# A hand-ordered list of steps in a fused mLSTM and channel-mix kernel: filling operand made first, first row fetched right behind its store, copies of unit 4's keys put behind chunk 7's scores and two row fetches

## The chip, the cores and the metric

The kernel runs on one core of one Trainium2 chip. A core has a matrix engine (PE), three engines for elementwise work (DVE, ACT, POOL) and a queue engine (SP) that here only issues transfers; ACT issues some transfers too. Each engine works through its own instructions in order and waits on semaphores that other engines and transfers raise. The metric is device microseconds of one execution, and the median over the runs is compared.

## The reference

Two layers follow each other. The first is an mLSTM over 4 batches, 8 heads, 768 steps and a head dimension of 40; the second is a channel mix on its output, with d_model 320 and d_ff 1024.

```python
m_new = np.maximum(f_gate[:, :, t] + m, i_gate[:, :, t])
f_stab = np.exp(f_gate[:, :, t] + m - m_new)
i_stab = np.exp(i_gate[:, :, t] - m_new)
C = f_stab[:, :, None, None] * C + i_stab[:, :, None, None] * np.einsum('bhd,bhe->bhde', vt, kt)
n = f_stab[:, :, None] * n + i_stab[:, :, None] * kt
h_tilde = np.einsum('bhde,bhe->bhd', C, qt)
denom = np.maximum(np.abs(nq), 1.0)          # nq = n . q
y[:, :, t] = sigmoid(o_gate) * h_tilde / denom
...
xk = mu_k * x + (1.0 - mu_k) * x_prev
xr = mu_r * x + (1.0 - mu_r) * x_prev
k = np.maximum(xk @ w_k, 0.0)
v = k * k @ w_v
out = sigmoid(xr @ w_r) * v
```

## The kernel before

The sequence is cut into 12 units of 256 tokens (3 for each batch) and each unit into 2 chunks of 128, so that there are 24 chunks. Within a chunk the mLSTM is a masked product: `scores` (line 471) multiplies keys by queries on PE, `exps` (464) makes the decay weights on ACT from a row that was fetched and masked, `weigh` (479) multiplies the two on DVE, and `intra` (504) multiplies the result by the values on PE. The state between chunks goes through `keys` (553), `carry` (568), `carry_out` (579) and `inter` (483). The channel mix of a unit is `turn` and `mix`, then `ffn_k`, `relu`, `sq`, `ffn_v` and `ffn_r`, each in float32 that is split into two parts, so that a product takes several matmuls.

All work is recorded in one list, `ORDER` (lines 51 to 203): each entry is a function's name and its arguments, a trailing letter naming the engine or queue (V is DVE, G POOL, A ACT, S SP). The order of the entries is the order of the instructions on every engine; no scheduler changes it. Transfers therefore stand in SP's row in the order of the list as well.

The steps that the prediction speaks of:

- `work` (296) writes the operand `busy` on DVE; `fill v n` (288) issues n matmuls of `busy` by `busy` whose result nobody reads. `zeros` (240) clears 32 rows of the buffers `k_first` and `q_first` on DVE.
- The gate scans of a segment c of 128 steps are `gate_b` (327), `gate_m` (338) and `gate_n` (349) on DVE, with `scale_a`, `scale_k` and `scale_d`. `turn_g` (369) transposes their rows on PE and `cols` (378) turns them into columns on ACT.
- `store_n c` (353) writes the row of segment c to a scratch tensor `nm` in device memory. `fetch_m g` (453) reads it back, 8 heads spread over all 128 partitions (512 KB), into one of two buffers `e`; `mask` (459) blanks the upper triangle on POOL. Segment c serves the chunks c, c+6, c+12 and c+18.
- The weights come by `load_w` (643), in four buffers, and go through `w_size` (650, ACT), `w_guard` and `w_bits` (657, 662, DVE), `w_h` (673, ACT) and `w_l` (677).
- `load_n`, `load_v`, `load_x`, `load_qs`, `load_o`, `load_cm` fetch a unit's keys, values, stacked queries or keys, gates, and the block mask of `carry_out`.
- Units 0 to 3 read keys and queries straight from `k_first` and `q_first`. From unit 4 on the stacks `k3` and `q3` are put together by `restack` (439): for the keys six copies of the high part (`restack u k h`), three of the low part (`k l`), and the same for the queries, 18 copies from buffer to buffer for a unit, all issued by SP. `k3` and `q3` have one buffer each, the same that `k_first` and `q_first` lie in, so unit 4's copies wait for the last scores of unit 3 (`scores 7 1`).

Of the kernel before, what the change touches and what calls it, by code (L numbers as in the profile page):

```python
# [14 lines left out]
B, H, S, D = 4, 8, 768, 40  # L15
# [33 lines left out]


ORDER = """
zeros V; consts; edge 0; load_i S; load_f A; gate_b 0; scale_a 0 G; load_w wk 0 A; gate_m 0; gate_n 0;
scale_k 0 V; load_n 0 S; blank; store_n 0 S; gate_b 1; work; load_w wk 1 A; gate_r 0; gate_i 1 V; gate_m 1;
scale_a 1 V; load_v 0 A; gate_n 1; scale_d 1 V; store_n 1 S; fill v 20; turn_g 0; cols 0; gate_r 1;
scale_k 1 G; fill v 13; turn_g 1; w_size wk 0; w_guard wk 0 V; w_bits wk 0 0; w_bits wk 0 1; w_bits wk 0 2;
load_mu A; gate_b 2; gate_i 2 V; gate_m 2; scale_a 2 G; gate_b 3; keys 0 G; gate_n 2; scale_d 2 V; cols 1;
keys 1 V; gate_r 2; gate_i 3 V; gate_m 3; load_x 0 q S; scale_k 2 V; gate_n 3; fill v 42; carry 0; load_cm S;
carry_out 0; w_size wk 1; scale_a 3 V; scale_k 3 V; fill v 10; carry 1; carry_out 1; fetch_m 0 S; fetch_m 1 S;
mask 0; w_h wk 0; exps 0 0; load_x 0 k S; w_l wk 0 V; store_n 2 S; w_guard wk 1 V; w_bits wk 1 0;
w_bits wk 1 1; fill v 6; turn_g 2; load_w wk 2 S; load_w wk 3 A; cols 2; carry_old 1 V; load_n 1 S; load_v 1 S;  # L60
gate_r 3; gate_b 4; gate_i 4 V; scale_a 4 G; fill v 10; scores 0 1; store_n 3 S; exps 0 1; scale_d 3 G;
load_o 0 S; gate_m 4; gate_n 4; scale_k 4 G; store_n 4 S; turn_g 3; cols 3; weigh 0 1; w_size wk 2; fill v 10;
scores 0 0; mask 1; exps 1 1; weigh 0 0; fill v 7; intra 0 0; gate_r 4; intra 0 1; w_bits wk 1 2; scores 1 0;
w_guard wk 2 V; w_bits wk 2 0; w_bits wk 2 1; w_bits wk 2 2; scores 1 1; scale_d 4 V; carry_add 1 V; keys 2 V;
load_qs 0 S; gate_b 5; gate_i 5 V; gate_m 5; fill v 10; carry 2; scale_a 5 V; carry_old 2 V; fetch_m 2 S;
gate_n 5; scale_k 5 G; inter 1; mask 2; w_h wk 1; w_h wk 2; exps 1 0; total 0; inter_v 1; w_size wk 3;
# [19 lines left out]
w_h wr 1; sq_l 0 0; turn 3; turned 3; mask 6; scores 6 0; w_guard wv 2 V; w_bits wv 2 0; w_l wr 0 V; intra 5 1;  # L86
w_l wr 1 V; scores 6 1; exps 6 0; weigh 6 0; change 1 G; load_qs 3 S; inter_v 5; total 5; exps 6 1; weigh 6 1;
norm 2 0; ffn_k 0 2; ffn_r 0 0; tanh_r 0 0; load_x 4 q S; split_h 4 q; sq_h 0 1; load_v 3 S; w_bits wv 2 1;
w_bits wv 2 2; intra 6 0; intra 6 1; load_o 2 S; norm 2 1; sq 0 1 A; restack 4 k h S; keys 7 V; scores 7 0;
norm 2 2; split_l 4 q V; carry 6; fetch_m 7 S; carry_out 6; ffn_r 0 1; mask 7; total 6; sq_l 0 1; mix 1 k;  # L90
tanh_o 2; sig_o 2; gate 2 G; outcome 2 G; restack 4 k l S; edge 2; tanh_r 0 1; fetch_m 8 S; scores 7 1;
exps 7 0; weigh 7 0; exps 7 1; weigh 7 1; ffn_k 0 3; relu 0 2; sq_h 0 2; mask 8; inter 7; inter_v 7; intra 7 0;
restack 4 q h S; restack 4 q l S; sq 0 2 V; load_n 4 A; twin 2; w_size wv 3; intra 7 1; total 7; norm 3 0;
norm 3 1; sq_l 0 2; load_v 4 S; w_guard wv 3 V; turn 4; mix_h 1 k; ffn_v 0 0 0; ffn_v 0 0 1; turned 4;
# [743 lines left out]
```

## Time and profile before

| | us |
|---|---|
| median of 3 runs | 394.19 |
| the three runs | 388.84, 394.19, 396.33 |
| the profiled execution, whole time | 396.55 |
| its span, first to last instruction | 394.8 |

| engine | busy us | share of the span |
|---|---|---|
| PE matmul | 359.2 | 91% |
| DVE | 273.5 | 69% |
| ACT | 220.5 | 56% |
| POOL | 114.8 | 29% |

PE's busy time contains the fillings, and it contains matmuls that ran while a lower clock was granted. The page cuts the span in 40 slices; the row of the granted clock stands in tenths, 9 being full.

```profile
PEclk9998967996759987999999999999999999999999
```

The slices with 5 to 8 lie in the first 160 us. After that the clock is full, and PE is nearly always busy.

### The profile page before, as it was taken

The page shows a single profiled execution, that of the slowest core. Times are in us where ns is not written, and L with a number is a line of the kernel's source. Part 1 is how long each engine was busy: PE and PEld are TensorE (multiplying, and loading weights), DVE is VectorE, ACT ScalarE, POOL GpSimd, SP SyncE. Part 2 cuts the span into 40 slices and gives each one's busy share as a digit, 9 for nine tenths or more (in the row PEclk, how much of TensorE's full clock was granted, in tenths as well). Part 3 has the DMA queues.
Part 4 walks back from the last instruction along what each step waited for, and adds up shares of the span by engine and source line. Part 5 has one row for each costly group of instructions (what it writes and reads, how often), then busy time and mean ns, then how long its engine had stood idle before and what let it go on. Part 6 is the DMA issues. An engine that isn't in the chain of part 4 may idle for free.

```text
span 394.8 us, 7334 instructions
## 1 busy us (share of the span) xinstructions
PE 359.2 (91%) x2721; PEld 352.6 (89%) x2721; DVE 273.5 (69%) x490; ACT 220.5 (56%) x491; POOL 114.8 (29%) x117
## 2 busy tenths in 40 slices
PE   2979989999179959989999999999999999999996
PEld 2969979989179949979999999999999999999896
DVE  6686978996068736749966778487769648675621
ACT  1334555574087845466775783666758564545460
POOL 2210343430042644425206644150044215001100
PEclk9998967996759987999999999999999999999999
DMA  7673859360559793765576547647650640000000
GB/s 234 206 261 123 282 182 358 127 195 2 175 166 279 210 250 100 189 221 184 176 240 211 171 127 201 184 144 192 192 167 27 196 150 0 35 2 35 0 35 33
DMA packets 33431, 61.82 MB, mean 157 GB/s; under 512 B 3419, under 2 KB 19091, under 8 KB 33075
## 3 DMA queue, kind: packets, MB, share of 16 engines
q1 hardware_dynamic: 29717, 52.36, 43.2%
q10 hardware_dynamic: 3678, 8.99, 7.4%
q8 instruction: 21, 0.34, 0.4%
q14 instruction: 15, 0.12, 0.1%
HBM read 41.58 MB, written 4.03 MB: 116 GB/s over the span
## 4 chain that ended last, share of the span: by engine, by line
PE 58%; DVE 19%; DMA 7%; ACT 6%; SPq 4%; issue 3%; POOL 1%; ACTq 0%; DVEq 0%; POOLq 0%
PE bv L752 15%; PE bpk L696 15%; PE bA L510 8%; PE bv L731 6%; PE bS L477 5%; SPq L449 4%; PE bv L294 2%; DMA re<-nm 2%; ACT re L469 2%; PE bT L576 2%; PE bT L596 2%; PE bA L492 2%; DVE rxm L622 2%; DVE re L481 1%; DMA rva<-va 1%
## 5 line engine op out<-in xcount | busy, mean ns | idle before, releaser
L752 PE MATMUL bv<-wvh,kx 128*128 128x320 f32 x384 | 94.0, 318 | 0.9 <-DVE kx L721 0.9
L696 PE MATMUL bpk<-rxl,wkh 128*128 128x256 f32 x288 | 76.2, 281 | 0.0
L469 ACT ACTIVATE re<-re,acol 128x128 f32<-128x128 f32 x192 | 60.0, 391 | 25.3 <-POOL re L461 25.1
L752 PEld LDWEIGHTS bv<-wvh,kx 128*128 128x128 f32 x384 | 66.8, 191 | 1.3 <-DVE kx L721 1.1
L510 PE MATMUL bA<-rva,re 128*128 128x41 f32 x384 | 49.9, 288 | 11.3 <-DVE re L481 10.8
L752 PE MATMUL bv<-wvl,kx 128*128 128x320 f32 x192 | 59.9, 312 | 0.0
L510 PEld LDWEIGHTS bA<-rva,re 128*128 128x128 f32 x384 | 48.4, 201 | 12.7 <-DVE re L481 11.6
L481 DVE TENSOR_TENSOR re<-bS,re 128x512 f32<-128x512 f32 x48 | 32.3, 683 | 38.9 <-PE bS L477 19.7
L696 PE MATMUL bpk<-rxh,wkh 128*128 128x256 f32 x192 | 55.5, 289 | 0.0
L696 PEld LDWEIGHTS bpk<-rxl,wkh 128*128 128x128 f32 x288 | 55.0, 191 | 0.0
L702 ACT ACTIVATE r<-bpk 128x512 f32<-128x512 f32 x48 | 28.2, 590 | 47.2 <-PE bpk L696 47.1
L461 POOL TENSOR_SCALAR_AFFINE_SELECT re<-re 128x1024 f32<-128x1024 f32 x24 | 28.3, 1181 | 89.7 <-DMA re<-nm 71.4
L696 PE MATMUL bpk<-rxh,wkl 128*128 128x256 f32 x192 | 53.8, 280 | 0.0
L721 DVE TENSOR_TENSOR kx<-bpk,kx 128x512 fp32r<-128x512 f32 x48 | 32.7, 683 | 16.0 <-ACT kx L707 11.7
L622 DVE SCALAR_TENSOR_TENSOR rxm<-rxd,mu_sb,rxT 128x256 f32<-128x256 f32 x72 | 39.0, 596 | 0.2
L294 PE MATMUL bv<-busy 128*128 128x256 f32 x201 | 32.4, 317 | 7.2 <-DVE R L345 7.2
L696 PEld LDWEIGHTS bpk<-rxh,wkh 128*128 128x128 f32 x192 | 36.8, 192 | 0.0
L752 PEld LDWEIGHTS bv<-wvl,kx 128*128 128x128 f32 x192 | 36.7, 191 | 0.0
L696 PEld LDWEIGHTS bpk<-rxh,wkl 128*128 128x128 f32 x192 | 36.7, 191 | 0.0
L294 PEld LDWEIGHTS bv<-busy 128*128 128x128 f32 x201 | 28.9, 218 | 7.4 <-DVE R L345 7.2
L707 ACT ACTIVATE kx<-r 128x512 fp32r<-128x512 f32 x48 | 29.8, 624 | 1.8 <-POOL rCn L588 1.0
L628 ACT ACTIVATE rxh<-rxm 128x768 fp32r<-128x768 f32 x24 | 20.1, 840 | 17.1 <-DVE rxm L622 16.9
(108 smaller groups left out, 700.8 us busy)
## 6 DMA issues: line engine op xcount, KB each, us to landing
re<-nm SPq DMA_DIRECT2D x18, 512.0 KB
rq<-qT SPq DMA_DIRECT2D x11, 360.0 KB
k<-rhk SPq DMA_DIRECT2D x32, 120.0 KB
q<-rhq SPq DMA_DIRECT2D x32, 120.0 KB
out<-rsg SPq DMA_DIRECT2D x12, 320.0 KB
ro<-og SPq DMA_DIRECT2D x11, 320.0 KB
re<-nm ACTq DMA_DIRECT2D x6, 512.0 KB
rva<-va SPq DMA_DIRECT2D x9, 328.0 KB
```

Source lines behind the costliest of these rows:

```text
L294: T.matmul(b[:, :U], busy[:, :P], busy, start=True, stop=True)
L461: G.affine_select(e, e, pattern=[[0, H], [1, L]], compare_op=ALU.is_ge, fill=NEG, base=0, channel_multiplier=-1)
L469: A.activation(e[:, h, :], e[:, h, :], AF.Exp, bias=acol[:, cc, bh.start + h:bh.start + h + 1])
L481: V.tensor_tensor(ev, ch[g]["S", i], ev, op=ALU.mult)
L510: T.matmul(ch[g]["I"][:, h * E1:(h + 1) * E1], ch[g]["e"][:, h, :], units[u]["va"][:, c, h * E1:(h + 1) * E1], start=True, stop=True)
L622: V.scalar_tensor_tensor(xm[:, ct, :], t["xd"][:, ct, :], mu_sb[:, i, ct:ct + 1], t["xT"][:, ct, :U], op0=ALU.mult, op1=ALU.add)
L696: T.matmul(pk[:, i * U:(i + 1) * U], p[part][:, ct, i * P:(i + 1) * P], xx[:, ct, :], start=n == 0, stop=n == len(tl) - 1)
L702: A.activation(r.rearrange("p i t -> p (i t)"), t["pk", pr], AF.Relu)
L707: A.activation(kh, t["r", pr], AF.Square)
L721: V.tensor_tensor(kl.rearrange("p i t -> p (i t)"), t["pk", pr], t["kh", pr].bitcast(F32).rearrange("p i t -> p (i t)"), op=ALU.subtract)
L731: T.matmul(pr[:, :DM], xx[:, ct, i * P:(i + 1) * P], W["wr", ct // 2][part][:, ct % 2, :], start=m == 0, stop=m == len(tl) - 1)
L752: T.matmul(t["pv", i][:, :DM], xx[:, j, ts], p[part][:, j, :], start=f == 0 and n == 0, stop=f == NF - 1 and n == 2)
```

## The change

Only the list changes; no function does. The three opening lines of the list show the first part:

```diff
-zeros V; consts; edge 0; load_i S; load_f A; gate_b 0; scale_a 0 G; load_w wk 0 A; gate_m 0; gate_n 0;
-scale_k 0 V; load_n 0 S; blank; store_n 0 S; gate_b 1; work; load_w wk 1 A; gate_r 0; gate_i 1 V; gate_m 1;
-scale_a 1 V; load_v 0 A; gate_n 1; scale_d 1 V; store_n 1 S; fill v 20; turn_g 0; cols 0; gate_r 1;
+work; fill v 22; zeros V; consts; edge 0; load_i S; load_f A; gate_b 0; scale_a 0 G; load_w wk 0 A; gate_m 0;
+gate_n 0; scale_k 0 V; blank; store_n 0 S; load_n 0 S; load_v 0 S; gate_b 1; gate_r 0; gate_i 1 V; gate_m 1;
+scale_a 1 V; gate_n 1; scale_d 1 V; store_n 1 S; fetch_m 0 S; load_w wk 1 S; turn_g 0; cols 0; gate_r 1;
```

Further on `fetch_m 0 S` is gone from its old place ahead of `fetch_m 1 S`, and `restack 4 k h S` has gone from ahead of `keys 7 V` to behind `scores 7 1`, where `restack 4 k l S` now follows it.

PE's row at the start of the program, before the change (`bv` is the bank that the fillings write, `bT` that of transposes and carries, `rar` the gate rows):

```order
L294 MATMUL bv_155<-busy 128x256 x20
L374 MATMUL bT_176<-ident,rar_121 128x32 x3
L294 MATMUL bv_155<-busy 128x256 x13
L374 MATMUL bT_176<-ident,rar_122 128x32 x3
L376 MATMUL bT_176<-rdg_151,ones 120x32
```

PE's row at the same place after it:

```order
L294 MATMUL bv_106<-busy 128x256 x22
L374 MATMUL bT_181<-ident,rar_145 128x32 x3
L294 MATMUL bv_106<-busy 128x256 x13
L374 MATMUL bT_181<-ident,rar_146 128x32 x3
L376 MATMUL bT_181<-rdg_172,ones 120x32
```

PE's row keeps its order, with 22 fillings for 20 at its head; what has moved is the writing of `busy`, from behind segment 0's scans to the head of DVE's row.

SP's row at the start of the program, before the change (`nm` is the scratch row, `re` a buffer `e`, `rkn` the keys, `rva` the values, `raw` weights):

```order
L316 DMA gi_sb<-gi 32x768
L411 DMA rkn_132<-kn 128x640
L354 DMA nm_77<-rar_121 32x128
L354 DMA nm_78<-rar_122 32x128
L395 DMA q_first<-qf 40x2048
L322 DMA cm_sb<-cmask 120x328
L456 DMA re_295<-nm_77 128x1024
L456 DMA re_296<-nm_78 128x1024
L395 DMA k_first<-kf 40x2048
```

SP's row at the same place after it:

```order
L316 DMA gi_sb<-gi 32x768
L354 DMA nm_77<-rar_145 32x128
L411 DMA rkn_161<-kn 128x640
L407 DMA rva_163<-va 128x656
L354 DMA nm_78<-rar_146 32x128
L456 DMA re_176<-nm_77 128x1024
L648 DMA raw_179<-wk 128x3x512
L395 DMA q_first<-qf 40x2048
L322 DMA cm_sb<-cmask 120x328
L456 DMA re_177<-nm_78 128x1024
L395 DMA k_first<-kf 40x2048
```

The keys' load now follows the first store, the values and the second piece of weights have come over from ACT's queue, and the first fetch stands ahead of that piece, of the queries and of the block mask.

SP's row around unit 4's copies, before the change (`k_4` and `q_4` are the stacks, `rhk` and `rhq` the high parts, `rk` and `rlq` the low parts):

```order
L415 DMA ro_360<-og 128x640
L449 DMA k_4_959<-rhk_839 40x3x256 x2
L449 DMA k_4_959<-rhk_839 40x2x256
L449 DMA k_4_959<-rhk_839 40x3x256 x2
L449 DMA k_4_959<-rhk_839 40x2x256
L456 DMA re_296<-nm_78 128x1024
L449 DMA k_4_959<-rk_782 40x3x256 x2
L449 DMA k_4_959<-rk_782 40x2x256
L456 DMA re_295<-nm_79 128x1024
L449 DMA q_4_1049<-rhq_942 40x3x256 x2
```

SP's row around the same copies after it:

```order
L415 DMA ro_362<-og 128x640
L456 DMA re_177<-nm_78 128x1024
L456 DMA re_176<-nm_79 128x1024
L449 DMA k_4_1002<-rhk_841 40x3x256 x2
L449 DMA k_4_1002<-rhk_841 40x2x256
L449 DMA k_4_1002<-rhk_841 40x3x256 x2
L449 DMA k_4_1002<-rhk_841 40x2x256
L449 DMA k_4_1002<-rk_784 40x3x256 x2
L449 DMA k_4_1002<-rk_784 40x2x256
L449 DMA q_4_1051<-rhq_944 40x3x256 x2
```

The two fetches (for chunks 7 and 8) stood behind and among the copies of the keys, and now stand ahead of all 18 copies of unit 4.

More of the change, by code (lines that the diff above doesn't have):

```diff
@@ L57 @@
 keys 1 V; gate_r 2; gate_i 3 V; gate_m 3; load_x 0 q S; scale_k 2 V; gate_n 3; fill v 42; carry 0; load_cm S;
[L58 to L63, printed above, removed]
+carry_out 0; w_size wk 1; scale_a 3 V; scale_k 3 V; fill v 10; carry 1; carry_out 1; fetch_m 1 S; mask 0;
+w_h wk 0; exps 0 0; load_x 0 k S; w_l wk 0 V; store_n 2 S; w_guard wk 1 V; w_bits wk 1 0; w_bits wk 1 1;
+fill v 6; turn_g 2; load_w wk 2 S; load_w wk 3 A; cols 2; carry_old 1 V; load_n 1 S; load_v 1 S; gate_r 3;
+gate_b 4; gate_i 4 V; scale_a 4 G; fill v 10; scores 0 1; store_n 3 S; exps 0 1; scale_d 3 G; load_o 0 S;
+gate_m 4; gate_n 4; scale_k 4 G; store_n 4 S; turn_g 3; cols 3; weigh 0 1; w_size wk 2; fill v 10; scores 0 0;
+mask 1; exps 1 1; weigh 0 0; fill v 7; intra 0 0; gate_r 4; intra 0 1; w_bits wk 1 2; scores 1 0;
 w_guard wk 2 V; w_bits wk 2 0; w_bits wk 2 1; w_bits wk 2 2; scores 1 1; scale_d 4 V; carry_add 1 V; keys 2 V;
@@ L88 @@
 norm 2 0; ffn_k 0 2; ffn_r 0 0; tanh_r 0 0; load_x 4 q S; split_h 4 q; sq_h 0 1; load_v 3 S; w_bits wv 2 1;
-w_bits wv 2 2; intra 6 0; intra 6 1; load_o 2 S; norm 2 1; sq 0 1 A; restack 4 k h S; keys 7 V; scores 7 0;
-norm 2 2; split_l 4 q V; carry 6; fetch_m 7 S; carry_out 6; ffn_r 0 1; mask 7; total 6; sq_l 0 1; mix 1 k;
-tanh_o 2; sig_o 2; gate 2 G; outcome 2 G; restack 4 k l S; edge 2; tanh_r 0 1; fetch_m 8 S; scores 7 1;
+w_bits wv 2 2; intra 6 0; intra 6 1; load_o 2 S; norm 2 1; sq 0 1 A; keys 7 V; scores 7 0; norm 2 2;
+split_l 4 q V; carry 6; fetch_m 7 S; carry_out 6; ffn_r 0 1; mask 7; total 6; sq_l 0 1; mix 1 k; tanh_o 2;
+sig_o 2; gate 2 G; outcome 2 G; edge 2; tanh_r 0 1; fetch_m 8 S; scores 7 1; restack 4 k h S; restack 4 k l S;
 exps 7 0; weigh 7 0; exps 7 1; weigh 7 1; ffn_k 0 3; relu 0 2; sq_h 0 2; mask 8; inter 7; inter_v 7; intra 7 0;
```

## The prediction, made before the changed kernel ran

> **What bounds the kernel now.** I read the page first, then SP's waits, then the timeline by engine at the two places that the diff touches, then the windows for the granted clock. From the page:
>
> ```profile
> span 394.8 us, 7334 instructions
> PE 359.2 (91%) x2721; PEld 352.6 (89%) x2721; DVE 273.5 (69%) x490; ACT 220.5 (56%) x491; POOL 114.8 (29%) x117
> ```
>
> PE is the engine to fill, so what the change is worth is PE's idle time and slow time in the first 125 us. The place in the middle, in the timelines of SP, POOL and PE (start, length; in brackets the idle time before and who ended it), with SP's longest wait from its list of waits:
>
> ```profile
> SPq L449 <- PE bS L477: 30.7, 4, 17.1
> 98.11 5.03 SPq L449 DMA_DIRECT2D k<-rhk  x6
> 103.67 0.34 SPq L456 DMA_DIRECT2D re<-nm  x1
> 104.14 2.46 SPq L449 DMA_DIRECT2D k<-rk  x3
> 107.25 4.88 SPq L449 DMA_DIRECT2D q<-rhq  x6
> 112.24 2.48 SPq L449 DMA_DIRECT2D q<-rlq  x3
> 123.23 4.90 SPq L449 DMA_DIRECT2D q<-rhq  x6
> 107.77 1.09 POOL L461 TENSOR_SCALAR_AFFINE_SELECT re<-re 128x1024 f32<-128x1024 f32 x1 [21.44 <-DMA re<-nm]
> 96.47 1.56 PE L477 MATMUL bS<-q_first,k_first 72*128 72x128 f32 x8
> 99.71 0.79 PE L492 MATMUL bA<-rCn,rq 120*128 120x123 f32 x6
> 111.02 3.64 PE L510 MATMUL bA<-rva,re 128*128 128x41 f32 x16 [10.51 <-DVE re L481]
> 118.44 0.78 PE L477 MATMUL bS<-q,k 120*128 120x128 f32 x3
> ```
>
> SP stands at the first key copy for 17.1 us, from 81.0, until chunk 7's last scores end at 98.0. The fetch of chunk 7's row is behind six copies, goes out at 103.67, is masked at 107.77, and PE, idle since 100.50, gets its `intra 7` at 111.02. Unit 4's first scores run at 118.44, and they need all 18 copies, whose issue ends at 114.72.
>
> The start, in the same view, PE first, then the others:
>
> ```profile
> 7.16 4.64 PE L294 MATMUL bv<-busy 128*128 128x256 f32 x20 [7.16 <-DVE R L345]
> 11.73 0.52 PE L374 MATMUL bT<-ident,rar 32*128 32x32 f32 x3
> 12.18 1.81 PE L294 MATMUL bv<-busy 128*128 128x256 f32 x13
> 14.43 5.29 PE L294 MATMUL bv<-busy 128*128 128x256 f32 x42
> 25.62 1.06 PE L477 MATMUL bS<-q_first,k_first 72*128 72x128 f32 x8
> 28.71 0.39 PE L376 MATMUL bT<-rdg,ones 32*120 32x32 f32 x2 [1.74 <-POOL rdg L367]
> 1.22 1.76 DVE L243 MEMSET k_first<- 32x2048 f32 x1 [1.22 <-PEq L829]
> 6.22 0.28 DVE L362 TENSOR_SCALAR rar<-rar 32x128 f32<-32x128 f32 x1
> 6.83 0.27 DVE L297 MEMSET busy<- 128x256 f32 x1
> 16.47 0.40 DVE L332 TENSOR_TENSOR_SCAN rbm<-ones,gf_sb 32x128 f32<-32x128 f32 x1
> 21.74 0.48 DVE L584 TENSOR_TENSOR rCn<-bT,cm_sb 120x328 f32<-120x328 f32 x1
> 8.37 0.64 POOL L362 TENSOR_SCALAR rar<-rar 32x128 f32<-32x128 f32 x1 [2.27 <-DVE rar L351]
> 18.40 1.08 POOL L461 TENSOR_SCALAR_AFFINE_SELECT re<-re 128x1024 f32<-128x1024 f32 x1
> 12.46 0.93 ACT L655 ACTIVATE rwf<-raw 128x768 f32<-128x768 f32 x1
> 14.82 0.93 ACT L655 ACTIVATE rwf<-raw 128x768 f32<-128x768 f32 x1
> 19.52 0.40 ACT L469 ACTIVATE re<-re,acol 128x128 f32<-128x128 f32 x1 [2.08 <-POOL re L461]
> 6.14 2.47 SPq L354 DMA_DIRECT2D nm<-rar  x2
> 12.62 0.83 SPq L456 DMA_DIRECT2D re<-nm  x2
> ```
>
> Segment 0's gate rows are ready at 6.50, yet PE transposes them at 11.73, since 20 fillings stand ahead that could not begin before `busy` was written. Everything behind follows that transpose: ACT's first `w_size` at 12.46, DVE's weight bits up to 16.47, POOL's mask at 18.40, `carry_out 0` at 21.74.
>
> The clock, from windows chosen around the slow stretches (window; length; busy time of PE, weight load, DVE, ACT, POOL with counts; granted clock; transfer share; GB/s):
>
> ```profile
> 2.00:12.00 10.00, 4.84 (x23) 4.62 (x23) 5.96 (x15) 1.28 (x1) 1.25 (x4) 1.00 0.85 283
> 14.00:18.00 4.00, 4.00 (x34) 3.96 (x35) 3.88 (x7) 2.05 (x5) 0.79 (x2) 1.00 0.98 299
> 29.00:33.00 4.00, 4.00 (x21) 3.97 (x21) 0.04 (x2) 2.46 (x8) 1.29 (x2) 0.57 0.42 129
> 53.00:63.00 10.00, 10.00 (x49) 9.71 (x49) 7.57 (x14) 3.23 (x10) 3.80 (x3) 0.51 0.54 176
> 100.50:105.00 4.50, 0.01 (x1) 0.00 (x0) 0.00 (x0) 0.00 (x0) 0.00 (x0) 0.93 0.42 138
> 105.00:111.00 6.00, 0.00 (x0) 0.00 (x0) 0.69 (x1) 2.11 (x8) 3.15 (x3) 0.50 0.75 253
> 111.00:118.00 7.00, 6.98 (x30) 6.98 (x31) 4.94 (x11) 5.68 (x16) 2.12 (x4) 0.50 0.55 157
> 118.00:124.00 6.00, 6.00 (x53) 5.90 (x52) 5.21 (x9) 3.91 (x7) 2.61 (x3) 1.00 0.90 257
> ```
>
> After 4 to 5 us of idling the clock is halved, and it then stays so for 4 to 10 us of busy PE (4, 10 and 7 in these rows).
>
> **Part 1, fillings first.** `busy` takes 0.27 at DVE's head, so PE begins at about 1.5. At the first group's pace, 4.64/20 = 0.232 each, 22 end at 6.6. DVE's chain to segment 0's rows starts 0.27 later and they are ready at 6.8; segment 1's rows are as before (9.01 on POOL), since the 0.27 is only moved ahead. So `turn_g 0` runs at 6.85 for 11.73: 4.9 earlier. The next 13 fillings take 1.74, `turn_g 1` finds its rows at 9.01, and the 42 fillings start near 9.6 for 14.43: 4.8 earlier. The two added fillings cost nothing while the rows come at 6.8; without that cover, 0.5. ACT's `w_size wk 0` goes from 12.46 to about 7.6, DVE's `gate_b 2` from 16.47 to 11.7, POOL's mask from 18.40 to 13.6, `carry_out 0` from 21.74 to 16.9, if their transfers are there.
>
> **Part 2, the transfers' order.** Loads of keys (320 KB) and values (328 KB) now go out behind the first store, at about 6.8. How long a transfer takes to begin I get from the fetch at 103.67: masked 4.1 later, of which 512 KB at 283 GB/s are 1.85, so at most 2.2 remain; data flow from about 8.9. Ahead of the block mask stand keys, values, the fetch (512), weights (768) and queries (320); with the mask's 154 that is 2402 KB or 2.46 MB, at 283 to 299 GB/s 8.2 to 8.7. The mask lands at 17.1 to 17.6, and `carry_out 0` is 4.1 to 4.6 earlier. The first fetch lands at about 13.0, in time for 13.6. The second weights land near 15.7, so ACT's second `w_size` is not earlier but later than 14.82, and `w_h` and `exps 0 0` behind it gain 2 instead of 4.8; they have slack, since `exps` is first wanted by DVE behind the scores at 25.62. `k_first` (with a second fetch, 852 KB more) lands between 20.3 and 23.2, the later value if ACT's fourth weight load takes half the rate; wanted at 21.3. Up to 1.74 of that lateness falls into the wait that PE has at 28.71 anyway. Bounds for parts 1 and 2: 4.8 gained, or, at the 176 GB/s of the 53 to 63 window, mask at 22.9 and 1.2 lost. I take 4.2 gained, by the rates of the same stage. Nothing from there to 98 depends on transfers that the change moves, so the shift is carried.
>
> **Part 3, the keys' copies behind the fetches.** Both fetches leave SP before the copies, as soon as their buffers are free (chunks 5 and 6, done before chunk 7's scores). POOL's row is idle for 21.44 there, so the mask costs nothing but some contention with DVE. `exps`, `weigh` and `intra 7` then follow the scores at about 100.5. What PE did from 111.02 to 118.44 at half clock, 7.4, takes 3.7 at full clock and ends near 104.5. But SP issues the 18 copies no faster: 5.03 + 2.46 + 4.88 + 2.48 with small gaps is 15.0, from 98.11 to 113.1 for 114.72. With 2.2 to land, unit 4's scores start at 115.3 for 118.44. PE has then idled 10.8, and the clock is halved as after the idle 10.5 of now; only now the slow stretch lies on the work behind the copies. The next gate is 123.23, when SP may begin unit 5's copies, after chunk 9's scores: 4.8 of full-clock work behind 118.44. From 115.3 it takes 4.8 plus half the slow stretch: 3.5 lost after 7 us (123.6), 2.0 after 4 us (122.1). I take the middle, 122.8: 0.4 gained. Bounds: 3.1 gained if the clock were full, 0.4 lost. So the hole of 10.5 is moved, not closed.
>
> [...]
>
> **The sum.** 4.2 + 0.4 = 4.6. The profiled execution took 396.55, so 391.95; that one lies 2.36 above the median of 394.19, so 389.6 for a median run.
>
> **The rivals.** First, the early store's write is slow to land: before, the stores went out at 6.14 and the fetch at 12.62, 6.5 later. If it is again 6.5, the fetch leaves at 12.9, and on SP the weights, queries and mask are queued behind it: 12.9 + 2.2 + 1754 KB at 290 GB/s (6.2) is 21.3, `carry_out 0` gains 0.4, and with part 3 the time is 393.4. For it speaks that row; against it, that SP's queue then held the keys ahead of it and ACT's two weight pieces and the values, at a share of 0.85 in the first window. [...]
>
> Second, the earlier start re-times the starved stretches and one slow stretch is missing, the largest being 53 to 63: 10.00 at 0.51 is 4.9 lost. Then 4.6 + 4.9 = 9.5 and 384.7. For it: how long the slow stretches last varies from 4 to 10. Against it: the order of PE's work and its waits are the same there.
>
> Third, on the other side: transfers at the lower rate starve PE ahead of `carry 1`. PE's fillings end at 14.9, and if the mask lands at 22.9 it has some 6 us of idling, the clock is halved, and 7 us of work at half clock cost 3.5: 1.2 + 3.5 - 0.4 is 4.3 lost, 398.5. It decides when the block mask lands after 21.74; against it are the rates of 283 and 299.
>
> **How the numbers follow.** Forecast 0.48, slow store 0.2, missing slow stretch 0.2, starved start 0.12. Range 384 to 395: it takes in the first three but the edges, and leaves out the last. About 2% (7.9 us) is what a measurement of this kernel can tell from no change. Faster by more means under 386.3: the second rival and little of the forecast, 0.22. Slower by more means over 402.1: 0.04. Within: 0.74.
>
> **What would show it.** Right: `turn_g 0` near 6.9, the first fetch issued near 9, `carry_out 0` near 17.4, chunk 7's scores near 94, and from there 17 us to unit 4's scores, at half clock. Part 3 wrong: unit 4's scores without a wait, or at full clock. Part 2 wrong: a first fetch after 12, or the mask after 20. The whole would be wrong if a new wait between 30 and 95 ate the shift.

## The result, and the profile after

The changed kernel takes 388.08 us by the median of 20 runs (382.65 to 399.03), beside 394.75 for the kernel before in the same session. The ratio is 0.986, 95% interval 0.982 to 0.990: 5.6 us less by the ratio and 6.7 by the medians, where 4.6 was forecast, and inside the 2% that the forecast called "within". Of the page of the profiled execution:

```profile
span 384.7 us, 7333 instructions
PE 358.0 (93%) x2723; PEld 351.1 (91%) x2723; DVE 275.0 (71%) x490; ACT 220.4 (57%) x491; POOL 115.5 (30%) x117
PEclk9969969989859989999999999999999999999999
```

The two profiled spans differ by 10.1 us, more than the medians do, so this pair overstates the change. PE is busy for 1.2 us less with two more instructions; 27.4 us of its busy time lie at half clock, 33.9 before. The start, in the timelines of PE, DVE, ACT and SP (start, length; in brackets the idle time before and what ended it):

```profile
1.18 5.06 PE L294 MATMUL bv<-busy 128*128 128x256 f32 x22 [1.18 <-DVE busy L297]
6.30 0.84 PE L374 MATMUL bT<-ident,rar 32*128 32x32 f32 x3
7.08 3.14 PE L294 MATMUL bv<-busy 128*128 128x256 f32 x13
10.87 5.28 PE L294 MATMUL bv<-busy 128*128 128x256 f32 x42
20.48 1.15 PE L576 MATMUL bT<-rva,rkt 128*120 128x123 f32 x6 [2.50 <-DVE rCn L584]
26.08 1.85 PE L477 MATMUL bS<-q_first,k_first 72*128 72x128 f32 x8
31.51 1.75 PE L510 MATMUL bA<-rva,re 128*128 128x41 f32 x14
19.93 0.50 DVE L584 TENSOR_TENSOR rCn<-bT,cm_sb 120x328 f32<-120x328 f32 x1 [3.08 <-DMA cm_sb<-cmask]
7.35 0.92 ACT L655 ACTIVATE rwf<-raw 128x768 f32<-128x768 f32 x1
18.45 0.89 ACT L655 ACTIVATE rwf<-raw 128x768 f32<-128x768 f32 x1 [7.07 <-DMA raw<-wk]
6.42 0.32 SPq L354 DMA_DIRECT2D nm<-rar  x1
8.70 0.43 SPq L456 DMA_DIRECT2D re<-nm  x1
```

PE reaches the first transposes at 6.30 (11.73 before), and the first fetch goes out at 8.70, 2.3 us behind its store. Then, in this execution, DVE waits 3.08 us for the block mask, and with it PE. The clock around that wait, from windows of the same trace (its record of the clock begins at 10.7 us, so that the 1.00 of the first row is not measured; window, length, busy time of PE, weight load, DVE, ACT, POOL, granted clock, transfer share, GB/s):

```profile
6.00:8.00 2.00, 1.87 (x9) 1.43 (x8) 1.79 (x7) 0.82 (x3) 0.38 (x3) 1.00 0.14 24
12.00:14.00 2.00, 2.00 (x19) 2.00 (x18) 1.97 (x5) 0.00 (x0) 1.24 (x2) 1.00 0.68 180
18.00:20.00 2.00, 0.00 (x0) 0.00 (x0) 0.07 (x1) 1.55 (x3) 0.00 (x0) 1.00 0.99 338
20.00:22.00 2.00, 1.52 (x9) 1.52 (x10) 1.22 (x4) 1.23 (x5) 0.00 (x0) 0.73 1.01 370
22.00:26.00 4.00, 4.00 (x20) 3.71 (x20) 3.93 (x9) 1.55 (x7) 0.00 (x0) 0.50 1.00 380
```

Between 6 and 8 us almost nothing is transferred (24 GB/s), since what was issued first is done and the store has only just gone. From 18 to 20 PE does nothing; from 20.9 its clock is halved. The middle, in the timelines of SP and PE, and two windows:

```profile
92.75 5.52 SPq L449 DMA_DIRECT2D k<-rhk  x6
98.32 2.39 SPq L449 DMA_DIRECT2D k<-rk  x3
100.82 4.83 SPq L449 DMA_DIRECT2D q<-rhq  x6
105.76 2.39 SPq L449 DMA_DIRECT2D q<-rlq  x3
117.41 4.91 SPq L449 DMA_DIRECT2D q<-rhq  x6
95.59 1.98 PE L510 MATMUL bA<-rva,re 128*128 128x41 f32 x16 [0.39 <-DVE re L481]
108.79 0.44 PE L477 MATMUL bS<-q,k 120*128 120x128 f32 x1 [8.78 <-DMA q<-rlq]
104.00:108.00 4.00, 0.00 (x0) 0.00 (x0) 0.00 (x0) 0.00 (x0) 0.00 (x0) 0.50 0.40 126
112.00:116.00 4.00, 4.00 (x21) 4.00 (x21) 0.43 (x1) 1.47 (x2) 0.00 (x0) 0.50 0.99 313
```

`intra 7` no longer waits (95.59, idle 0.39, for 10.51). PE's hole now lies ahead of unit 4's first scores, 8.78 us long, while SP issues the copies; from 104 to 108 every engine is idle. The hole was moved and is 1.7 us shorter.

**How these times scatter.** The record of the granted clock in the traces of before and after holds 0.50 or 1.00, and its stretches at 0.50 last 3.41, 6.83, 10.24 or 13.65 us: one to four steps of 3.41. The stretches at half clock (us) in four profiled executions:

```
before   29.3-32.7  53.2-63.4  90.7-97.5  104.4-118.0  145.3-152.2
after    20.9-27.7  51.6-58.5  82.3-85.8  102.8-116.5  140.4-143.8
e2_keys             51.2-58.0  88.8-92.2  102.4-116.1  140.0-143.4
e3_fill  27.4-41.0  54.7-61.5             99.1-116.1   140.0-146.8
```

As far as unit 4's copies e2_keys (below) is the same program as the kernel before; without the stretch at 29.3 it reaches `intra 0` at 31.37, the kernel before at 33.73. Each run lists its mean clock, so the time at half clock is 2 x (1 - clock) x span. Over 150 runs of this study one line fits, with a constant for each kernel: span = constant + 0.444 x time at half clock, residual 1.8 us. The table gives both: a ratio leaves out the runs over 1.5% above the fastest of their kernel (in e2, e3 and e9 it rests on two of six) and is taken beside the kernel before in the same session, while the means are of all runs whose clock is listed (with standard error).

| kernel | runs | ratio, 95% interval | mean us | us at half clock | against before, at equal half-clock time |
|---|---|---|---|---|---|
| before | 46 | 1 | 395.0 ± 0.6 | 42.2 | 0 |
| after | 20 | 0.986 (0.982 to 0.990) | 388.8 ± 0.8 | 38.6 | -4.7 ± 0.5 |
| e1_start | 12 | 0.990 (0.985 to 0.996) | 390.6 ± 0.8 | 43.7 | -5.1 ± 0.6 |
| e2_keys | 6 | 0.981 (0.972 to 0.990) | 391.3 ± 1.3 | 37.8 | -1.8 ± 0.8 |
| e3_fill | 6 | 0.969 (0.960 to 0.977) | 386.7 ± 1.5 | 36.5 | -5.7 ± 0.8 |
| e12_order | 6 | not given | 396.5 ± 1.9 | 43.5 | +0.9 ± 0.8 |
| e7_fillkeys | 6 | 0.972 (0.964 to 0.979) | 386.1 ± 1.4 | 34.9 | -5.7 ± 0.8 |
| e4_mask | 6 | 0.973 (0.966 to 0.980) | 388.8 ± 2.2 | 40.6 | -5.5 ± 0.8 |
| e5_hole | 6 | 0.978 (0.972 to 0.984) | 386.6 ± 0.9 | 30.9 | -3.5 ± 0.8 |
| e9_hole70 | 6 | 0.985 (0.973 to 0.997) | 388.5 ± 1.7 | 34.0 | -2.8 ± 0.8 |
| e6_work | 6 | 0.972 (0.964 to 0.980) | 387.6 ± 2.3 | 39.2 | -6.1 ± 0.8 |
| e8_queues | 6 | 0.982 (0.975 to 0.990) | 390.3 ± 1.3 | 44.7 | -5.9 ± 0.8 |
| e10_all | 12 | 0.987 (0.976 to 0.997) | 385.2 ± 0.9 | 30.7 | -4.7 ± 0.6 |
| e11_nofill | 6 | 0.985 (0.977 to 0.993) | 386.3 ± 2.0 | 35.6 | -5.8 ± 0.8 |

### The profile page after: what moved, and what is told of

It is laid out like the page before. It is cut to its first block, busy times and chain, and to the rows that moved or that the text cites. A ratio compares the mean times of both kernels' runs of the same rounds, so it can differ in the third digit from the quotient of the medians.

```text
span 384.7 us, 7333 instructions
## 1 busy us (share of the span) xinstructions
PE 358.0 (93%) x2723; PEld 351.1 (91%) x2723; DVE 275.0 (71%) x490; ACT 220.4 (57%) x491; POOL 115.5 (30%) x117
## 4 chain that ended last, share of the span: by engine, by line
PE 57%; DVE 17%; DMA 12%; SPq 5%; ACT 5%; issue 3%; POOL 0%; ACTq 0%; DVEq 0%; POOLq 0%
PE bpk L696 17%; PE bv L752 16%; PE bA L510 7%; PE bv L731 5%; PE bS L477 5%; SPq L449 5%; DMA q<-rlq 3%; DMA cm_sb<-cmask 2%; DVE rxm L622 2%; PE bv L294 2%; PE bT L576 2%; PE bA L492 2%; ACT re L469 2%; DVE re L481 2%; DMA re<-nm 2%
## 5 line engine op out<-in xcount | busy, mean ns | idle before, releaser
L752 PE MATMUL bv<-wvh,kx 128*128 128x320 f32 x384 | 92.8, 315 | 0.9 <-DVE kx L721 0.9
L696 PE MATMUL bpk<-rxl,wkh 128*128 128x256 f32 x288 | 77.9, 286 | 0.2 <-DVE rxl L639 0.2
L469 ACT ACTIVATE re<-re,acol 128x128 f32<-128x128 f32 x192 | 60.0, 390 | 10.9 <-POOL re L461 10.7
L696 PEld LDWEIGHTS bpk<-rxl,wkh 128*128 128x128 f32 x288 | 56.4, 196 | 0.4 <-DVE rxl L639 0.4
L461 POOL TENSOR_SCALAR_AFFINE_SELECT re<-re 128x1024 f32<-128x1024 f32 x24 | 28.1, 1170 | 72.8 <-DMA re<-nm 19.9
L510 PE MATMUL bA<-rva,re 128*128 128x41 f32 x384 | 47.7, 281 | 0.9 <-DVE re L481 0.8
L510 PEld LDWEIGHTS bA<-rva,re 128*128 128x128 f32 x384 | 46.5, 194 | 2.1 <-DVE re L481 1.1
L622 DVE SCALAR_TENSOR_TENSOR rxm<-rxd,mu_sb,rxT 128x256 f32<-128x256 f32 x72 | 40.8, 621 | 0.2
L294 PE MATMUL bv<-busy 128*128 128x256 f32 x203 | 34.8, 331 | 1.2 <-DVE busy L297 1.2
L477 PE MATMUL bS<-q,k 120*128 120x128 f32 x128 | 20.6, 291 | 13.1 <-DMA q<-rlq 9.8
L294 PEld LDWEIGHTS bv<-busy 128*128 128x128 f32 x203 | 31.2, 232 | 1.4 <-DVE busy L297 1.2
L477 PEld LDWEIGHTS bS<-q,k 120*128 120x128 f32 x128 | 18.4, 207 | 14.7 <-DMA q<-rlq 9.7
```

What stands on the lines that cost most here:

```text
L294: T.matmul(b[:, :U], busy[:, :P], busy, start=True, stop=True)
L461: G.affine_select(e, e, pattern=[[0, H], [1, L]], compare_op=ALU.is_ge, fill=NEG, base=0, channel_multiplier=-1)
L469: A.activation(e[:, h, :], e[:, h, :], AF.Exp, bias=acol[:, cc, bh.start + h:bh.start + h + 1])
L477: T.matmul(pS[:, j * L:(j + 1) * L], t["k3"][:, h, cs], t["q3"][:, h, cs], start=True, stop=True)
L510: T.matmul(ch[g]["I"][:, h * E1:(h + 1) * E1], ch[g]["e"][:, h, :], units[u]["va"][:, c, h * E1:(h + 1) * E1], start=True, stop=True)
L622: V.scalar_tensor_tensor(xm[:, ct, :], t["xd"][:, ct, :], mu_sb[:, i, ct:ct + 1], t["xT"][:, ct, :U], op0=ALU.mult, op1=ALU.add)
```

## The experiments

### The change taken apart: e1_start, e2_keys, e3_fill, e12_order, e7_fillkeys

e1 is the kernel before with the first two parts (the start of the diff, and the first fetch gone from its old place); e2 is the third part alone (of the changed lines only the part that matters is shown, here and below):

```diff
-norm 2 1; sq 0 1 A; restack 4 k h S; keys 7 V; scores 7 0;
+norm 2 1; sq 0 1 A; keys 7 V; scores 7 0;
...
-outcome 2 G; restack 4 k l S; edge 2; tanh_r 0 1; fetch_m 8 S; scores 7 1;
+outcome 2 G; edge 2; tanh_r 0 1; fetch_m 8 S; scores 7 1; restack 4 k h S; restack 4 k l S;
```

> The kernel before with the first two parts only (fillings first; first row fetch behind its store and the transfers in their new order), unit 4's copies where they were. Theory A, what the changed kernel's trace suggests: these parts carry nearly all of the gain, about 2 us of it by 33 us and more where the stretches at half clock behind them come out shorter: 388 to 391 us against 394.75, ratio 0.983 to 0.991; carry_out 0 near 20, intra 0 near 31.5, chunk 7's last scores near 93, 98.1 then copies as before and a 10 us hole ahead of them near 83 to 93. Theory B, that the moved copies carry the gain: 393 us or more, ratio 0.995 to 1.003.

> The kernel before with the third part only (copies of unit 4's keys behind two row fetches and chunk 7's scores); its start is as before. Theory A: the copies still take some 15 us of issue behind chunk 7's scores and nothing else is left to cover them, so the hole is moved: start of unit 5's copies 0.4 us earlier than 123.23, time 393.8 to 395 us, ratio 0.998 to 1.001. Theory B: the closed hole at 88 to 98 is gained: 388 to 391 us, ratio 0.983 to 0.99.

e1 measured 0.990 and e2 0.981. Both gain, so neither theory held as it was put: A is right about e1's time (B's range is touched only at its lower end), B about e2's ratio. But e2's median, 392.91, lies above B's times; by the means e2 gains 3.7 ± 1.4, at equal half-clock time 1.8 ± 0.8. Two of A's places were missed in e1's trace: `intra 0` ran at 34.01 and chunk 7's scores ended at 95.72, with four halved steps from 19.7 to 33.3, where the changed kernel with the same start had two. The trace of e2 shows the mechanism of A nevertheless: unit 5's copies start 24.2 us behind chunk 7's last scores, 25.2 in the kernel before, so one microsecond is gained there. The rest comes behind that point, and is taken up below.

e3 has the first part alone, e12 the second alone, and e7 is the changed kernel without its second part:

```diff
-zeros V; consts; edge 0;
+work; fill v 22; zeros V; consts; edge 0;
...
-gate_b 1; work; load_w wk 1 A;
+gate_b 1; load_w wk 1 A;
...
-store_n 1 S; fill v 20; turn_g 0;
+store_n 1 S; turn_g 0;
```

> The kernel before with the first part only (operand and 22 fillings first; the transfers in their old order and on their old queues). Theory A: TensorE reaches carry 0 near 16 but the block mask lands near 20 to 21.7 as before, and the first fetch is issued no earlier than before, so TensorE stands idle about 5 us ahead of carry 1 and the clock is halved there: intra 0 between 33 and 35, time 393 to 398 us, ratio 0.996 to 1.008. Theory B, that the fillings alone give the gain: intra 0 near 31.5, 388 to 391 us, ratio below 0.991.

> The kernel before with the second part only (transfers in the new order, fetch 0 behind its store, second weights on SyncE's queue; the fillings where they were). Theory A, this order gains nothing by itself since the block mask lands at 19.5 to 20.5 and TensorE reaches carry 1 only near 21: intra 0 within 1 us of the 31.4 to 33.7 seen with the old start, time 393 to 396.5 us, ratio 0.995 to 1.003. Theory B, as the forecast had it, the order brings 1 to 4 us: 390.5 to 393.5 us, ratio 0.987 to 0.995.

> The changed kernel with the transfers of its first 20 us in the old order and on the old queues (fillings first and unit 4's copies behind the fetches are kept). Theory A, the new order of the transfers gained nothing because the block mask then lands later (19.93 against 18.56 with the fillings alone): carry_out 0 near 18.6, first fetch near 11, scores 0 1 near 22.5, intra 0 near 30; time 385 to 388 us, ratio 0.973 to 0.984, no slower than the changed kernel. Theory B, the early first fetch is worth what the forecast put on it: intra 0 near 32 or later, time 389 to 392, ratio 0.986 to 0.994.

e3 gains at least what e1 gains: 0.969, by the means 3.9 ± 1.7 more, at equal half-clock time 0.6 ± 0.9 more. Theory A fell there. In the timelines of DVE and PE of e3:

```profile
18.56 0.48 DVE L584 TENSOR_TENSOR rCn<-bT,cm_sb 120x328 f32<-120x328 f32 x1
19.09 0.86 PE L576 MATMUL bT<-rva,rkt 128*120 128x123 f32 x6 [1.68 <-DVE rCn L584]
30.12 3.47 PE L510 MATMUL bA<-rva,re 128*128 128x41 f32 x16
7.02 1.81 PE L294 MATMUL bv<-busy 128*128 128x256 f32 x13
```

With the transfers in their old order `carry_out 0` runs at 18.56, not at 19.93 as in the changed kernel, and PE waits 1.68 instead of 2.50. That the new order delays the mask is not shown by this pair. Of six traces with the new order behind early fillings, whose program is the same up to there, `carry_out 0` ran at 18.37 (e8) and 18.53 (e6) in two and at 19.82 to 20.11 in four (e1, e9, after, e5); with the old order it ran at 18.56 and 17.93 (e7). The mean is 1.2 us later, but one and the same start differs by more from execution to execution. e12 gains nothing (median 398.36 beside 393.12; `carry_out 0` at 21.27 for 21.74, first fetch at 8.67 for 12.62). Its median lies above even A's range. e7 is A's case: `carry_out 0` at 17.93, first fetch at 11.56, `intra 0` at 29.91, 386.1. So the second part does what it says, the fetch is 2.4 to 4 us earlier, and brings no time. Three pairs differ by it alone: with it the mean is higher by 3.9 ± 1.7 (e1, e3), 2.7 ± 1.6 (after, e7) and 1.5 ± 2.0 (e12, before), at equal half-clock time by 0.6 to 1.0.

### The block mask earlier: e4_mask

```diff
-load_i S; load_f A;
+load_i S; load_cm S; load_f A;
...
-fill v 42; carry 0; load_cm S; carry_out 0;
+fill v 42; carry 0; carry_out 0;
```

> The changed kernel with one transfer moved: the block mask (154 KB) is fetched behind the first gate rows instead of behind the first queries. Theory A, the block mask is what holds carry_out 0 and with it leaves TensorE idle and its clock halved from 20.6 to 27.3: carry_out 0 near 17 instead of 19.93, the half-clock stretch behind it gone or shorter, scores 0 1 before 24 instead of 26.08, intra 0 at 29 to 30.5 instead of 31.51; time 384 to 387 us, ratio 0.973 to 0.981. Theory B, another transfer (second weights at 18.45, the first rows) ends as late as the mask: intra 0 within 0.5 us of 31.51, time within 1 us of the changed kernel's, ratio 0.983 to 0.988.

From the timelines of DVE and PE of this run:

```profile
16.78 0.48 DVE L584 TENSOR_TENSOR rCn<-bT,cm_sb 120x328 f32<-120x328 f32 x1
24.93 0.39 PE L376 MATMUL bT<-rdg,ones 32*120 32x32 f32 x2 [2.91 <-POOL rdg L367]
29.85 1.98 PE L510 MATMUL bA<-rva,re 128*128 128x41 f32 x16
```

The block mask was what held `carry_out 0`: it runs 3.2 us earlier, PE's wait there is gone, chunk 0's scores begin at 20.66 instead of 26.08, and `intra 0` is 1.7 us earlier. The wait went to the next thing that is late, POOL's diagonal for segment 3 (2.91), and one halved step follows it at 25.7 to 29.2. The ratio, 0.973, is at A's edge and beside the changed kernel's 0.986, but the means are equal (388.8 and 388.8 ± 2.2). That the 1.7 us reach the end is not shown. They do not reach chunk 7's scores, which end at 91.68, and at 91.57 in e6, which has the changed kernel's start and as much time at half clock up to there (13.7 us).

### The hole ahead of unit 4's scores: e5_hole, e9_hole70, e6_work, e8_queues

```diff
-turn 5; turned 5; w_bits wv 3 0; w_bits wv 3 1; scores 8 0;
+turn 5; turned 5; w_bits wv 3 0; w_bits wv 3 1; fill pk 60; scores 8 0;
```

> The changed kernel with 60 fillings (about 8.3 us at full clock) put into TensorE's hole between turn 5 (100.0) and unit 4's first scores (108.79). Theory A, the copies' issue sets when the scores begin and the clock is halved from 102.8 to 116.5 because TensorE stands idle ahead of them: unit 4's scores begin 16.1 us behind chunk 7's last as now, but the clock is full from there, and the 8.6 us from those scores to the start of unit 5's copies become 5 to 6: 2 to 3.5 us gained there, time 384.5 to 386.5 us by the median of 388.08 (ratio to before 0.972 to 0.98). Theory B, the work behind the copies is bound by something else than TensorE's clock: those 8.6 us stay above 8, time as the changed kernel's, ratio 0.983 to 0.988. Theory C: the clock is halved there whatever TensorE does: halved windows at 102 to 117 as now.

In PE's timeline and the windows of e5:

```profile
102.51 7.44 PE L294 MATMUL bpk<-busy 128*128 128x256 f32 x60
112.06 0.33 PE L477 MATMUL bS<-q,k 120*128 120x128 f32 x1 [2.11 <-DMA q<-rlq]
112.00:116.00 4.00, 3.41 (x14) 3.16 (x15) 1.38 (x2) 0.00 (x0) 0.00 (x0) 0.52 0.91 247
```

The fillings were too short by 2.1 us, and the clock was halved for two steps from the moment that the scores began. Theory C fell (four steps became two). A and B were left undecided: the 8.25 us from the scores to unit 5's copies are B's, the time of 386.57 is nearly A's. So the same with `fill pk 70`:

> The changed kernel with 70 fillings in the hole behind unit 4's copies (the 60 before took 7.44 us, left TensorE idle for 2.1 us, and the clock was halved for two stretches of 3.4 us from the moment that the scores began). Theory A, TensorE's clock binds the work behind the copies: with 8.7 us of fillings no stretch is halved between 100 and 120, and from unit 4's first scores to the start of unit 5's copies it takes 5 to 6.5 us instead of 8.6; time 384 to 386 us, ratio 0.972 to 0.98. Theory B, the order of the work behind the scores binds it, not the clock: 7.5 us or more there, time 386 to 388.5 us.

```profile
100.07 8.64 PE L294 MATMUL bpk<-busy 128*128 128x256 f32 x70
110.42 0.30 PE L477 MATMUL bS<-q,k 120*128 120x128 f32 x1 [1.71 <-DMA q<-rlq]
```

One step stayed halved (112.8 to 116.2), and from unit 4's first scores to unit 5's copies it took 7.22 us, where after, e2, e4 and e7, with four halved steps there, took 8.1 to 8.6. Three steps fewer are worth 0.9 to 1.4 in this stage: nearer B. As the scores begin 16.8 us behind chunk 7's here, 0.7 later, 0.2 to 0.7 are left at unit 5's copies. The time is unclear (median 390.08, the interval holds both). At equal half-clock time the fillings lose 1 to 2 us against the changed kernel.

In e6 ready work goes into the hole instead:

```diff
-w_bits wv 3 1; scores 8 0; w_bits wv 3 2; w_h wv 2; scores 8 1; ffn_k 1 0; weigh 8 0; carry 7; scores 9 1;
+w_bits wv 3 1; ffn_k 1 0; carry 7; scores 8 0; w_bits wv 3 2; w_h wv 2; scores 8 1; weigh 8 0; scores 9 1;
```

> The changed kernel with work that is ready put into the same hole instead of fillings: ffn_k 1 0 and carry 7 ahead of unit 4's first scores instead of behind them. Theory A: 16 + 6 products leave the half-clock stretch behind the copies (3.5 us and 1.4 us long there) and take 2.7 us of the 8.8 us hole, so the 8.6 us from unit 4's first scores to unit 5's copies become 4 to 6: 2.5 to 4.5 us gained there, time 383.5 to 386 us (ratio 0.969 to 0.978). Theory B, other engines or transfers hold that stage: unit 5's copies still start 24 to 25 us behind chunk 7's scores, ratio 0.983 to 0.988.

From the timelines of PE and SP of e6, and a window:

```profile
107.58 0.44 PE L477 MATMUL bS<-q,k 120*128 120x128 f32 x1 [4.94 <-DMA q<-rlq]
108.46 3.98 PE L477 MATMUL bS<-q,k 120*128 120x128 f32 x15 [0.43 <-DMA q<-rlq]
112.97 4.91 SPq L449 DMA_DIRECT2D q<-rhq  x6
136.40 0.42 PE L731 MATMUL bv<-wrh,rxl 128*128 128x320 f32 x1 [2.17 <-DVE rxl L639]
116.00:120.00 4.00, 4.00 (x19) 4.00 (x20) 1.06 (x3) 1.32 (x4) 1.92 (x2) 0.50 0.68 174
```

Here theory A holds in its place: from the scores to unit 5's copies it takes 5.39 us, all at half clock (five steps, 104.8 to 121.8). So the order of PE's work sets that stage, and its clock only adds to it. But it is given back: from unit 5's copies to unit 6's it takes 28.35 us, 24.2 in e7 and e9. The half clock now lies there: 8.8 us of it fall behind unit 5's copies, with PE busy all the time, which at half the pace would cost 4.4 (half of 8.8, an estimate), and the difference is 4.1; e7 and e9 have no halved step in this stage. The new wait of 2.17 at 136.40 was followed by none. Behind chunk 7's scores unit 6's copies start after 49.75 us, in e7 after 48.5, in the changed kernel after 51.6.

e8 puts the `l` copies, `restack 4 k l` and `restack 4 q l`, on ACT's queue behind `exps 7 1`:

> The changed kernel with 6 of unit 4's 18 copies issued by ScalarE behind its exponentials of chunk 7, the other 12 by SyncE. Theory A, the 0.8 us that each copy takes to issue on one queue sets when unit 4's scores begin: SyncE is done 10 us behind chunk 7's scores, ScalarE's six take 5 us out of its own work and delay turn 4 and turn 5 by 4 us, so unit 4's scores begin 11.5 to 13 us behind chunk 7's last instead of 16.1, and the start of unit 5's copies is 2 to 4.5 us earlier: time 384 to 386.5 us, ratio 0.971 to 0.98. Theory B, what sets it is the landing of the copies in shared transfer engines: unit 4's scores begin 15 us or more behind, ratio 0.983 to 0.99.

SP's and ACT's queue in e8:

```profile
96.20 6.21 SPq L449 DMA_DIRECT2D k<-rhk  x6
102.52 6.02 SPq L449 DMA_DIRECT2D q<-rhq  x6
99.28 3.26 ACTq L449 DMA_DIRECT2D q<-rlq  x3
```

While two queues issue, SP's first six take 6.21 us and ACT's last three 3.26, for 5.52 and 2.39 in the changed kernel, where SP issues alone. Behind SP's seventh lies a gap of 1.2 us, when ACT's are all out; why is not known. SP's 12 end 12.4 us behind chunk 7's scores, not 10, and `turn 4`, behind ACT's delayed work, comes after 6.45 us of idle PE. Unit 4's scores come 15.5 us behind, unit 5's copies 24.2: theory B by its numbers, though not for its reason alone.

### What gained, together: e10_all, e11_nofill

e7's start with e4's block mask; in the hole 50 fillings, then `ffn_k 1 0` and `carry 7` (e10), or those two alone (e11).

> What gained, together: fillings first with the transfers in their old order, the block mask behind the first gate rows, unit 4's copies behind the fetches, and in the hole 50 fillings, ffn_k 1 0 and carry 7 ahead of unit 4's first scores. Theory A: carry_out 0 near 16.7, intra 0 near 29.5; scores 16 us behind chunk 7's last, unit 5's copies 4.5 to 5.5 us behind those; no halved stretch between 100 and 118; time 380 to 383.5 us, ratio 0.963 to 0.973. Theory B, the gains do not add (each only moves where the clock is halved): 385 to 388 us, ratio 0.975 to 0.984.

> As the run with all of it, without the 50 fillings in the hole. Theory A: the clock is halved for four to five stretches of 3.4 us from about 103, and the time is 1 to 3 us above the run with all of it. Theory B, the clock there costs nothing because the stage is bound by copies and fetches: the same time within 1 us.

By the ratio neither is shown to beat the changed kernel. By the mean of all runs e10 is 3.6 ± 1.2 below it (385.2, 12 runs; 388.8, 20 runs), and at equal half-clock time it is the same (-4.7 for both): it spends 30.7 us at half clock instead of 38.6. `carry_out 0` ran only at 18.03, so the early mask bought little beside the old order. In the hole theory A holds (unit 5's copies come 5.3 us behind unit 4's first scores), but the clock was halved from 111.2 to 121.4 all the same, and by the time e10 is nearer its B. e11 has four halved steps there (106.5 to 120.1), as A has it, and differs from e10 by no more than its error, as B has it: what the fillings bring there stays open.

## Why the prediction was right, point by point

**The sum** was 4.6; at equal half-clock time 4.7 ± 0.5 was measured. The other microsecond or two would be halved steps that fell away (42.2 to 38.6 us, times 0.444 is 1.6 ± 0.9, which can be chance). Of the two terms, the start (4.2) is -4.4 ± 1.0 by e1 against before and -2.5 ± 1.5 by after against e2. The traces tell it more sharply: chunk 7's last scores end at 98.04 before and at 94.66 in e3, each with 20.5 us at half clock ahead of them. Over the 14 traces that end fits 88.6 + 0.449 x this half-clock time (residual 0.4), and lies 3.3 ± 0.3 earlier where the fillings stand first. So the shift is carried that far, as the forecast said, and is 0.9 smaller. The moved copies (0.4) are -3.7 ± 1.4, -1.8 ± 1.1 and -0.6 ± 2.1 by e2 against before, after against e1, and e7 against e3, some 2 us; at equal half-clock time they are -1.8 ± 0.8, 0.4 ± 0.7 and 0.0 ± 1.0. That the sum agrees so well is in part luck: the start is worth less than forecast, the copies bring more by the means, at a place that the forecast did not look at, and part 2 brings nothing.

**Part 1** stands, and is the whole of the start's gain (e3). `turn_g 0` came at 6.30 (6.85 forecast), ACT's first `w_size` at 7.35 (7.6), the mask of chunk 0 at 14.20 (13.6). The 13 fillings took 3.14 instead of 1.74, 0.24 each: the pace of the ten that take 2.50 from 23.78 on, at clock 0.50. In e3 they took 1.81.

**Part 2**: the fetch left at 8.70, near the 9 that was forecast, and the slow store did not come true. That it could leave some 2 us behind its store no run had shown (12.62 for stores at 6.14 before); here it follows by 2.28 us. The step "The mask lands at 17.1 to 17.6" failed: 19.9, and the second weights at 18.4 for 15.7. The rate was right on the whole: 287 GB/s from 8.9 to 19.9, uneven (180 from 12 to 14, 347 from 14 to 16). But 3.16 MB went through in that time, where the forecast counted 2.46 MB up to the mask. It put the second fetch, `k_first` and a third piece of weights behind the mask; they were issued at 11.05, 11.60 and 14.47, and by these figures 0.7 MB of them went through before the mask was there. Why, no run shows. The new order was to bring the mask forward and does not (the traces under e3); at the end of chunk 7's scores it makes 0.2 ± 0.3 us, on the later side, by the same 14 traces.

**The starved start** came true in part. Its point of decision, a mask after 21.74, was set too late: at 19.9 PE already had 2.5 us of idling and two halved steps. It cost what the mechanism said in place, chunk 0's scores being later than before (26.08 for 25.62), but not the whole gain. In other executions of the same start it cost less: in e6 and e8 these scores came at 22.43 and 22.27.

**Part 3**: "So the hole of 10.5 is moved, not closed" held: 16.1 us from chunk 7's scores to unit 4's (17 forecast), 8.78 of them idle, the clock at 0.50 from 102.8 to 116.5. POOL's masks of chunks 7 and 8 ran ahead of it, at 86.39 and 94.54, for 1.09 and 1.35 us. What contention with DVE can be stands in the trace of the kernel before: at 61.47 a mask took 1.73, and DVE's L671 beside it 1.60, for 0.81 at 59.64. The gain at unit 5's copies was 0.4 forecast, and is 0.5 by the profiled pair (25.2 to 24.7) and 1.0 by the mean of four traces without the part (before, e1, e3, e12: 25.4) and four with it (after, e2, e4, e7: 24.3). What failed is the step "The next gate is 123.23", with which the sum stopped. In the stage behind it PE waits for the first scores of unit 5. Before, and in e7:

```profile
145.18 0.32 PE L477 MATMUL bS<-q,k 120*128 120x128 f32 x1 [2.81 <-issue]
```

```profile
135.34 0.30 PE L477 MATMUL bS<-q,k 120*128 120x128 f32 x1 [1.28 <-issue]
```

The longest idle ahead of those scores, the halved steps behind it and the time from unit 5's copies to unit 6's mostly go together:

```
              idle    halved steps   unit 5's to unit 6's copies
e12_order     3.59    2              29.4
e1_start      3.07    2              29.1
before        2.81    2              29.4
after         1.94    1              26.9
e2_keys       1.65    1              26.8
e4_mask       1.52    1              26.3
e7_fillkeys   1.28    0              24.2
e9_hole70     1.00    0              24.2
```

All without the moved copies have two steps there (e3 too: 1.84, two, 27.3), all with them one or none. (In e6, e10 and e11, with PE's work in another order, an idle of 1.95 to 2.17 comes earlier and no halved step follows it; their 27.7 to 28.4 us begin with 8.2 to 8.9 at half clock, left from the stretch before.) So the part gained a microsecond up to 123 and some 2.5 us behind it in these traces: one halved step less, at most 1.7 of it (half of 3.41), and a wait that is about 1 us shorter. This is the rival of the "missing slow stretch", at another place than the one named (53 to 63) and for another reason: a shorter wait ahead of it. Why the wait is shorter was not tried; fetch 9 leaves 6.8 us ahead of unit 5's copies instead of 3.4, but that is not it alone, since e9 has 5.3 with an idle of 1.00 and e12 5.6 with one of 3.59.

**The half clock behind the copies** lasted 7.7 us from unit 4's scores on (108.8 to 116.5), with PE busy for 7.2 of them; the forecast reckoned with 7 or 4 and took the middle.

## What to carry to other kernels

A gain that ends in front of a wait is not finished there: follow it to the next engine that stands idle, and look whether a halved step comes behind it: here idles of 1.28 us without one and 1.94 us with one lie in stages of 24.2 and 26.9 us. Where a transfer is put first, list what it is put ahead of: here an early fetch that nobody waited for went ahead of a small mask that PE waited for, and gained nothing. Where one trace of each kernel tells a story, look for others with the same code at that place: here the same start gave waits and halved steps as different as those between the kernels. Where runs of one kernel differ by 4% (382.65 to 399.03 here), compare kernels also at equal time at half clock, or a change of 1% can be the chance of where the clock was halved.

## What the hardware showed that was not expected

- Not only idles of 4 to 5 us were followed by a halved step. Ahead of unit 5's scores idles of 1.52 (e4), 1.65 (e2) and 1.94 us (after) were followed by one and 1.84 (e3) by two, those of 1.28 (e7) and 1.00 (e9) by none; at another place those of 1.95 to 2.17 (e11, e10, e6) by none. In the kernel before the clock was halved from 90.7 on, and the longest idle in the 14 us ahead was 0.68, at 87.46: the length alone does not decide. After the idle of 8.78 us in the changed kernel 7.7 us passed at half clock, 7.2 with PE busy.
- The first fillings ran at about half the pace of the later ones. In the changed kernel 22 took 5.06 us from 1.18 on and 13 took 3.14 from 7.08 on (0.23 and 0.24 each), the 42 from 10.87 on 5.28 (0.13); its record of the clock begins at 10.7, at full. In e3, where the 22 took 5.06 too, the 13 took 1.81 (0.14).
- While SP and ACT issued unit 4's copies at once, in e8, six took 6.21 us on SP and three 3.26 on ACT; where SP issued them alone, in the changed kernel, six took 5.52 and three 2.39.
